# An adaLN block with a spectral network and a SwiGLU network: the gate modulation and the first gate weights are computed inside the first network, and its last shrunk rows and first output rows come in another order

## The chip, the cores and the metric

One core of a Trainium2 chip runs the whole program. The metric is the device time of one execution in microseconds (us). Three executions of the kernel before were timed, and its figure is their median, 1454.27 us. A profile comes from one further execution, recorded by the hardware profiler. The engines are named as in the profile: PE is the matrix engine and PEld its weight loads, DVE the vector engine, ACT the scalar (activation) engine, POOL the GpSimd engine and SP the engine that here only issues DMAs. SPq, ACTq and POOLq are the DMA queues of those engines.

## The reference

The input x has 4096 tokens (one row of a 1 x 4096 image) of 640 channels, all in float32. With silu(a) = a * sigmoid(a):

```
mod = (silu(c) @ w_mod).reshape(c.shape[0], 6, 1, -1)
sa, ca, ga, sb, cb, gb = mod[:, 0], mod[:, 1], mod[:, 2], mod[:, 3], mod[:, 4], mod[:, 5]
h = layernorm(x) * (1 + ca) + sa
x = x + ga * A(h)        # first network
h = layernorm(x) * (1 + cb) + sb
x = x + gb * B(h)        # second network
```

A is a spectral network: a real FFT over the 4096 tokens, a complex two-layer perceptron in four blocks of 160 channels on each frequency (ReLU between the layers), a soft shrinkage by 0.01 of the real and the imaginary parts, and the inverse FFT. B is SwiGLU: (silu(h @ w_gate) * (h @ w_up)) @ w_down, with 1728 hidden columns. c is one row of 640 values, so each of the six modulations is one row of 640 values. In this text they are numbered m = 0 to 5: sa, ca, ga, sb, cb, gb. The last, gb, is the gate modulation of the title.

## The kernel before

Matrix products whose float32 inputs have to be kept exact are split: an operand becomes a rounded high part, copied by ACT, and a low part, which is the operand minus the high part, formed by DVE. Three matmuls (high by high, low by high, high by low) then take the place of one.

**First network.** The FFT is done as matmuls with DFT tables. The middle of the network runs over 8 chunks of frequencies with 4 steps each, 32 steps p = 0 to 31 that are written out by hand in program order; each engine works through its own instructions in this order. `LAST` is 28, the first step of the last chunk. In one step, `stage_l1` and `tail_l1` do the first layer of a block, `stage_l2` the second layer of the block before, and a row of frequencies that is a few steps older is moved by DMA (`move_x`), shrunk (`shrink`, on DVE, two operations at L812 and L813 in the last chunks), split (`shrink_high` on ACT at L819, `shrink_low` on DVE at L824), multiplied by the first inverse table (`stage_i`, L835 to L837), copied by ACT (L838) and stored to a scratch array `s2` in DRAM by POOL's queue (L839). Rows are counted in the same numbers as steps; the last loop handles rows 24 to 26, and rows 25 to 27 are finished behind it. Rows 28 to 31, of the last chunk, go another way: `shrink_last` and `inverse_last`, whose copies `cz` are stored by ACT's queue for the first half of the channels (hf = 0) and by POOL's for the second (hf = 1).

**Modulations.** The rows of w_mod are loaded in 5 pieces of 128 x 640 for each m. DVE multiplies piece k by a column of silu(c) and adds it up in the tile `acc` (`mod_add`, L553 and L555); then `mod_sum` sums over the partitions by matmuls against ones. For m = 0, 2, 3, 4 this is put into the loop over p by the tables `mods` and `sums`, five pieces in every six steps. m = 1 is done ahead of the loop. m = 5 (gb) is not in the loop: `gate_load`, `gate_add`, `gate_sum` and `gate_out` (L1595 to L1619) do it at the start of the second network.

**First output rows.** Behind the loop, `first_y(i, hf)` forms the outputs of the first four rows i = 0 to 3 of tokens for the two halves hf of the channels: matmuls with the table `et` against the rows read back from `s2` (`cfrm`, `cfrr`; L1035 for hf = 0, L1040 for hf = 1) and against `tt` (L1038, hf = 1). DVE multiplies by ga, POOL or DVE adds x, and `first_stats` and `first_norm` give the normalised rows `xn`. The order of the eight is the list `order` at L1069. After them come `inverse_last` for hf = 1 (L885), the 20 transposes of `xn` (L1890), and `first_g`.

**Second network.** The 4096 tokens are 6 tiles; tile 0 has 512 token columns. For each tile the hidden columns are worked off in blocks of 256: a gate block, an up block, and so on, with the remainder of 64 columns of both as a third set. The sets of weights of tile 0 are numbered n in the order gate 0, up 0, remainder, gate 1, up 1, gate 2, ...; `load_w` loads set n into a raw tile r0_n (L1375, or L1378 and L1379 for the remainder) by SP, and `prep_w` makes its high (L1393) and low (L1396) parts in wb0_n, of which there are two buffers. `first_g` (L1884) evaluates set 0: it splits the transposed rows into ht (high, L1892, and low, L1895, by way of hx, L1894) and runs 30 matmuls of 512 columns. The following sets are run by `plain` (L1942 to L1944). A row of weights of w_down (`wdr`) is multiplied by gb on POOL (`fold`, L1559) and split. Beside this, tile 0 finishes the rest of the first network's output, row by row (r = 4, 5, ...: `row_load`, L1659 chh, L1662 chl, the matmuls py at L1672).

Here the order is not written by hand. A planner builds it while the program is generated: pieces of work are `Step`s with an engine, an estimated duration, the keys that they need and the buffers that they take; they stand in chains, and the planner puts the next step of a chain in place when its estimated time on its engine comes. `core("A", t)` and `core("V", t)` tell it how long ACT and DVE are taken by work outside the chains.

## Time and profile before

| | |
|---|---|
| three timed executions | 1447.88, 1454.27, 1458.53 us |
| median | 1454.27 us |
| profiled execution, its own time | 1457.64 us |
| its span, from the first to the last instruction | 1455.9 us |
| mean granted clock of PE | 0.995 |
| PE busy | 1410.7 us, 97% |
| DVE, ACT, POOL busy | 1089.2, 785.8, 543.6 us |
| DMA, mean | 260 GB/s |

Times in the views below are microseconds from the start of the span. A row of a timeline gives the start, the duration, the engine, the line, the operation and the tiles (out<-in); x7 at its end is the number of instructions put together in the row, and a bracket gives the idle time of the engine just before it and what ended it. The second network starts at about 312 us, where the transposes of `xn` begin, and the first down projection (`pd`) of tile 0 starts at 354.56 us.

### The profile page before, as it was taken

The numbers are of one execution on the slowest core, as the hardware profiler recorded it, in microseconds if no ns is written. First come the engines' busy times: TensorE is split into PE (matmuls) and PEld (weight loads), VectorE is DVE, ScalarE is ACT, GpSimd is POOL, SyncE is SP. The second block draws the span as 40 slices with busy tenths as digits, with TensorE's granted clock in tenths as the row PEclk, the third lists the DMA queues.
The fourth block names the chain that finished last, engine by engine and source line by source line (L and its number), as shares of the span: only waits on it lengthen the run. The fifth ranks groups of instructions, "written<-read, shape, count | busy, mean of one in ns | idle before, by whom it ended". The sixth has DMA issues, their size and how long they took to land.

```text
span 1455.9 us, 23927 instructions
## 1 busy us (share of the span) xinstructions
PE 1410.7 (97%) x8516; PEld 1331.4 (91%) x8516; DVE 1089.2 (75%) x1974; ACT 785.8 (54%) x1559; POOL 543.6 (37%) x640
## 2 busy tenths in 40 slices
PE   6899999988999999999999999999999999999998
PEld 2699999856888888899999999999999999999998
DVE  8868777768787788757878868778747767567775
ACT  7858888644544555544565456555435445244432
POOL 5300100145545344322544423444324545046532
PEclk9999999999999999999999999999999999999999
DMA  9978677557677988798987997877796666966652
GB/s 379 319 239 256 205 210 234 182 185 237 224 280 259 333 302 276 277 371 288 314 271 250 347 377 253 302 246 242 241 350 215 219 218 239 351 210 233 205 186 86
DMA packets 186136, 379.00 MB, mean 260 GB/s; under 512 B 22145, under 2 KB 104001, under 8 KB 184225
## 3 DMA queue, kind: packets, MB, share of 16 engines
q1 hardware_dynamic: 177824, 361.09, 72.4%
q0 software_dynamic: 6608, 13.77, 3.0%
q10 hardware_dynamic: 1584, 2.62, 0.5%
q8 instruction: 67, 1.10, 0.3%
q14 instruction: 53, 0.43, 0.1%
HBM read 263.39 MB, written 104.86 MB: 253 GB/s over the span
## 4 chain that ended last, share of the span: by engine, by line
PE 75%; DVE 10%; DMA 7%; ACT 3%; issue 2%; POOL 2%; SPq 1%; DVEq 0%; ACTq 0%; POOLq 0%
PE pd L2399 13%; PE pw L2078 8%; PE pw L2080 8%; PE pw L2079 7%; PE pc L777 4%; PE pd_X L2259 4%; PE pl L709 4%; PE pg L1942 2%; PE pg L1943 2%; PE pg L1944 2%; PE pd_Y L2259 2%; PE pw L2089 2%; PE pw L2091 2%; PE pw L2090 2%; DMA cr<-s 2%
## 5 line engine op out<-in xcount | busy, mean ns | idle before, releaser
L2399 PE MATMUL pd<-wdh,a 128*128 128x320 f32 x1040 | 239.2, 310 | 1.4 <-DVE x L2371 0.8
L2399 PEld LDWEIGHTS pd<-wdh,a 128*128 128x128 f32 x1040 | 176.2, 188 | 2.6 <-DVE x L2371 1.0
L1396 DVE TENSOR_TENSOR wb<-r,wb 128x512 fp32r<-128x512 f32 (+3 forms) x156 | 160.3, 1035 | 19.4 <-ACT wb L1393 17.3
L2399 PE MATMUL pd<-wdl,a 128*128 128x320 f32 x540 | 166.2, 309 | 0.0
L2078 PE MATMUL pw<-h,wt 128*128 128x384 f32 x416 | 141.0, 339 | 2.0 <-ACT s_y L2097 1.2
L2080 PE MATMUL pw<-h,wt 128*128 128x384 f32 x416 | 140.4, 337 | 0.0
L2079 PE MATMUL pw<-h,wt 128*128 128x384 f32 x416 | 139.9, 336 | 0.0
L2371 DVE TENSOR_TENSOR x<-x,pd 128x320 f32<-128x320 f32 x240 | 109.0, 478 | 37.8 <-PE pd L2399 33.9
L1393 ACT ACTIVATE wb<-r 128x512 fp32r<-128x512 f32 (+3 forms) x172 | 117.9, 703 | 34.4 <-PE pw L2091 24.9
L2080 PE MATMUL pw<-h,wb 128*128 128x384 f32 x312 | 105.1, 337 | 2.3 <-DVE wb L1396 2.3
L2078 PE MATMUL pw<-h,wb 128*128 128x384 f32 x312 | 105.3, 337 | 0.0
L2079 PE MATMUL pw<-h,wb 128*128 128x384 f32 x312 | 104.8, 336 | 0.0
L1942 PE MATMUL pg<-ht,wb 128*128 128x512 f32 x260 | 103.6, 398 | 1.3 <-ACT wb L1393 1.3
L1944 PE MATMUL pg<-ht,wb 128*128 128x512 f32 x260 | 102.2, 393 | 2.2 <-DVE wb L1396 2.2
L1943 PE MATMUL pg<-ht,wb 128*128 128x512 f32 x260 | 102.0, 392 | 0.0
L2399 PEld LDWEIGHTS pd<-wdl,a 128*128 128x128 f32 x540 | 101.4, 188 | 0.5
L2097 ACT ACTIVATE s_x<-pw 128x384 f32<-128x384 f32 x52 | 25.4, 489 | 114.0 <-PE pw L2080 113.3
L1655 POOL TENSOR_TENSOR cr<-cr,gab 128x640 f32<-128x640 f32 x28 | 48.0, 1715 | 98.6 <-DMA cr<-s 89.6
L839 POOL DMA_DIRECT2D s<-co x28 | 15.7, 562 | 181.8 <-ACT co L838 174.0
L2078 PEld LDWEIGHTS pw<-h,wt 128*128 128x128 f32 x416 | 78.4, 188 | 3.7 <-ACT s_y L2097 2.3
L2079 PEld LDWEIGHTS pw<-h,wt 128*128 128x128 f32 x416 | 78.5, 189 | 0.0
L2080 PEld LDWEIGHTS pw<-h,wt 128*128 128x128 f32 x416 | 78.3, 188 | 0.0
(346 smaller groups left out, 4057.6 us busy)
## 6 DMA issues: line engine op xcount, KB each, us to landing
wt<-td SPq DMA_DIRECT2D x104, 512.0 KB, 5.3
hs<-ho SPq DMA_DIRECT2D x52, 512.0 KB, 4.9
h<-hs SPq DMA_DIRECT2D x32, 768.0 KB, 9.3
r<-in_B_w_gate_dram SPq DMA_DIRECT2D x36, 640.0 KB, 5.2
r<-in_B_w_up_dram SPq DMA_DIRECT2D x36, 640.0 KB, 5.4
wdr<-wdd SPq DMA_DIRECT2D x21, 640.0 KB, 5.1
td<-wt SPq DMA_DIRECT2D x25, 512.0 KB, 5.8
g<-s SPq DMA_DIRECT2D x7, 1280.0 KB, 7.6
```

Source lines behind the costliest of these rows:

```text
L709: mm(pls[g][:, :NN], *seqs[g][i], start=(i == 0), stop=(i == n - 1))
L1393: act.activation(wbs[t, n][:, 0, ks, e], raw[t, n][:, ks, e], AF.Copy)
L1396: (pool if onp else dve).tensor_tensor(wbs[t, n][:, 1, ks, e], raw[t, n][:, ks, e], f32(wbs[t, n][:, 0, ks, e]), op=OP.subtract)
L1942: mm(b, wh, hh, start=(kk == 0), stop=False)
L1943: mm(b, wh, hl, start=False, stop=False)
L1944: mm(b, wl, hh, start=False, stop=(kk == 4))
L2078: mm(b, w(0, kp), a[:, kp, 0], start=start and kp == 0, stop=False, skip_group_check=not start)
L2079: mm(b, w(0, kp), a[:, kp, 1], start=False, stop=False, skip_group_check=not start)
L2080: mm(b, w(1, kp), a[:, kp, 0], start=False, stop=kp == 1, skip_group_check=not start)
L2259: mm(bk[b, i][:, :320], x, y, start=new and j == 0, stop=j == len(seq) - 1, skip_group_check=not new)
L2371: dve.tensor_tensor(x2[:, e], x2[:, e], x[0][:, :320], op=OP.add)
L2399: mm(pd[g, hf][0][:, :320], l, m, start=i == 0, stop=i == len(s) - 1 and not (last and len(gs) > 1))
```

## The change

It has four parts.

1. The modulation gb (m = 5) joins the other four in the loop of the first network. The pieces come one in each step from p = 2 on (loads) and p = 4 on (adds), where they came five in six steps; the sums stand at p = 9, 14, 19, 24 and 29, and the two halves of ga are now summed in the same step. The gate steps of the second network go.
2. The first gate weights (set 0) are loaded a second time, early: `first_gate` at p = 30 loads them by SP into two raw tiles (wr4, wr1) behind the load of x2_0. `first_gate_high` makes the high parts on ACT behind the loop, `first_gate_low` the low parts on DVE ahead of the first output rows. `first_g` uses these. wb0_0 is not made any more; its raw tile r0_0 is still loaded, since sums of weights for later tiles are formed from it, but behind r0_1 and r0_2. Two of the five hx tiles are made by DVE in place of ACT, and the planner is told 5.6 and 5.3 us in place of 7.7 and 7.4.
3. Row 27 is shrunk on POOL at p = 30 (`shrink_pool`) in place of DVE behind the loop, and at p = 31 the splits of row 26 and the high part of row 27 are moved forward, around `tail_l1`.
4. The list `order` has another order, and the statistics and norms of rows move with it.

The core of the diff:

```diff
+            gbb = []
...
-            for i, m in enumerate((0, 2, 3, 4)):
+            for i, m in enumerate((0, 2, 3, 4, 5)):
                 for k in range(5):
-                    mods.setdefault(3 + 6 * i + k, []).append((mod_load, m, k))
-                    mods.setdefault(5 + 6 * i + k, []).append((mod_add, m, k))
-                sums.setdefault(11 + 6 * i if m < 4 else LAST, []).append((mod_sum, m, 1))
-                if m == 2:
-                    sums.setdefault(10 + 6 * i, []).append((mod_sum, m, 0))
+                    mods.setdefault(2 + 5 * i + k, []).append((mod_load, m, k))
+                    mods.setdefault(4 + 5 * i + k, []).append((mod_add, m, k))
+                if m in (2, 5):
+                    sums.setdefault(9 + 5 * i, []).append((mod_sum, m, 0))
+                sums.setdefault(9 + 5 * i, []).append((mod_sum, m, 1))
...
+            def first_gate():
+                src = wg.rearrange("(k p) f -> p k f", p=P)
+                wraw.append(hp.tile([P, 4, 256], F32, tag="rz", bufs=2, name="wr4"))
+                wraw.append(p2.tile([P, 256], F32, tag="wm", bufs=1, name="wr1"))
+                nc.sync.dma_start(wraw[0], src[:, 0:4, 0:256])
+                nc.sync.dma_start(wraw[1], src[:, 4, 0:256])
+            def first_gate_high():
+                for k in range(5):
+                    act.activation(wh[k], wraw[0][:, k] if k < 4 else wraw[1], AF.Copy)
+            def first_gate_low():
+                for k in range(5):
+                    dve.tensor_tensor(wl[k], wraw[0][:, k] if k < 4 else wraw[1], f32(wh[k]), op=OP.subtract)
+            def shrink_pool(n):
+                xx = xxs[n // 4, n % 4]
+                pool.tensor_scalar(acc, xx, LAM, -LAM, op0=OP.min, op1=OP.max)
+                pool.tensor_tensor(xx, xx, acc, op=OP.subtract)
...
             for p in range(LAST + 1, NP):
+                last = p == NP - 1
...
+                if last:
+                    on(shrink_high, p - 5)
+                    on(shrink_low, p - 5)
                 on(tail_l1, p)
+                if last:
+                    on(shrink_high, LAST - 1)
...
                     load_first()
-                on(shrink_high, p - 5)
+                    first_gate()
+                    shrink_pool(LAST - 1)
...
-            on(shrink, LAST - 1)
-            on(shrink_high, LAST - 1)
+            first_gate_high()
             on(stage_i, LAST - 2)
...
-            order = [(0, 1), (1, 1), (0, 0), (1, 0), (2, 0), (3, 0), (2, 1), (3, 1)]
+            order = [(0, 1), (1, 1), (2, 1), (0, 0), (1, 0), (2, 0), (3, 0), (3, 1)]
...
-                    act.activation(x, pts[k], AF.Identity, bias=sb1[:, k:k + 1], scale=cb1[:, k:k + 1])
+                    if k < 3:
+                        act.activation(x, pts[k], AF.Identity, bias=sb1[:, k:k + 1], scale=cb1[:, k:k + 1])
+                    else:
+                        dve.tensor_scalar(x, pts[k], cb1[:, k:k + 1], sb1[:, k:k + 1], op0=OP.mult, op1=OP.add)
...
-                core("A", 7.7)
-                core("V", 7.4)
+                core("A", 5.6)
+                core("V", 5.3)
```

What it does to the order of the instructions is shown at three places. The first is PE among the first output rows, before; py0_i_hf is the output of row i and half hf.

```order
L1040 MATMUL py0_1_1_3837<-cfrm_3085,et_3284 128x320
L1035 MATMUL py0_0_0_3846<-cfrm_3085,et_3284 128x320
L1035 MATMUL py0_1_0_3851<-cfrm_3085,et_3284 128x320
L1035 MATMUL py0_2_0_3863<-cfrr_3086,et_3284 128x320
L1035 MATMUL py0_3_0_3875<-cfrr_3086,et_3284 128x320
L1038 MATMUL py0_2_1_3880<-tt7_0_3547,et_3284 128x320 x2
L1038 MATMUL py0_2_1_3880<-tt7_1_3558,et_3284 128x320 x2
L1040 MATMUL py0_2_1_3880<-cfrr_3086,et_3284 128x320
```

And the same place of the changed program:

```order
L1082 MATMUL py0_1_1_3879<-cfrm_3104,et_3303 128x320
L1080 MATMUL py0_2_1_3888<-tt7_0_3575,et_3303 128x320 x2
L1080 MATMUL py0_2_1_3888<-tt7_1_3586,et_3303 128x320 x2
L1082 MATMUL py0_2_1_3888<-cfrr_3105,et_3303 128x320
L1077 MATMUL py0_0_0_3897<-cfrm_3104,et_3303 128x320
L1077 MATMUL py0_1_0_3902<-cfrm_3104,et_3303 128x320
L1077 MATMUL py0_2_0_3912<-cfrr_3105,et_3303 128x320
L1077 MATMUL py0_3_0_3924<-cfrr_3105,et_3303 128x320
```

The five matmuls of row 2's second half moved ahead of the four outputs that read the first half of `cfrm` and `cfrr`.

The second place is SP's queue between the two networks, before; r0_n are the raw weight tiles, gwm the pieces of w_mod for gb, wdr the first rows of w_down, cr4 and x4 the inputs of row 4.

```order
L1375 DMA r0_0_3944<-in_B_w_gate_dram 128x5x256
L1375 DMA r0_1_3965<-in_B_w_up_dram 128x5x256
L1378 DMA r0_2_3967<-in_B_w_gate_dram 128x5x64
L1379 DMA r0_2_3967<-in_B_w_up_dram 128x5x64
L1597 DMA gwm0_3952<-in_w_mod_dram 128x640
L1597 DMA gwm1_3971<-in_w_mod_dram 128x640
L1597 DMA gwm2_3973<-in_w_mod_dram 128x640
L1597 DMA gwm3_3975<-in_w_mod_dram 128x640
L1597 DMA gwm4_3953<-in_w_mod_dram 128x640
L1552 DMA wdr0_0_3959<-in_B_w_down_dram 128x2x640
L1375 DMA r0_3_4065<-in_B_w_gate_dram 128x5x256
L1375 DMA r0_4_4085<-in_B_w_up_dram 128x5x256
```

After the change the same queue reads (the tiles named cr0_0 and x0_0 hold row 4's inputs):

```order
L1417 DMA r0_1_3994<-in_B_w_up_dram 128x5x256
L1420 DMA r0_2_3987<-in_B_w_gate_dram 128x5x64
L1421 DMA r0_2_3987<-in_B_w_up_dram 128x5x64
L1417 DMA r0_0_4009<-in_B_w_gate_dram 128x5x256
L1594 DMA wdr0_0_4002<-in_B_w_down_dram 128x2x640
L1650 DMA cr0_0_3995<-s2 128x640
L1646 DMA x0_0_3996<-in_A_x_dram 128x640
L1417 DMA r0_3_4116<-in_B_w_gate_dram 128x5x256
L1417 DMA r0_4_4118<-in_B_w_up_dram 128x5x256
L1613 DMA wdd<-wdr0_0_4002 128x1280
L1650 DMA cr5_4161<-s2 128x640
L1646 DMA x5_4170<-in_A_x_dram 128x640
```

The five gwm loads are gone, r0_0 stands behind r0_1 and r0_2, and row 4's inputs moved ahead of r0_3. Of the two buffers of its tag, r0_3 takes the one that r0_0 had in the program before, and so waits for the low part of wb0_0; now it takes that of r0_2, and waits for the low part of wb0_2.

The third place is ACT behind `first_g`, before; sg are the silus of the first gate block, wb0_n the high parts, a0 the high part of silu times up, wt the summed weights for later tiles, chh4 the high part of row 4.

```order
L1964 ACTIVATE sg0_0_0_3962<-pg0_0_3984 128x512
L1964 ACTIVATE sg0_0_1_4070<-pg0_1_3985 128x512
L1393 ACTIVATE wb0_1_4072<-r0_1_3965 128x512
L1393 ACTIVATE wb0_1_4072<-r0_1_3965 128x768
L1393 ACTIVATE wb0_2_4083<-r0_2_3967 128x2x128
L1450 ACTIVATE wt0_0a_3951<-ts0_3950 128x2x256
L1393 ACTIVATE wb0_2_4083<-r0_2_3967 128x3x128
L1619 ACTIVATE gbb_3960<-gpm0_4116 128x320
L1619 ACTIVATE gbb_3960<-gpm1_4118 128x320
L1978 ACTIVATE a0_0_0_0_3954<-sg0_0_0_3962 128x512
```

And after the change:

```order
L1435 ACTIVATE wb0_1_3982<-r0_1_3994 128x512
L1435 ACTIVATE wb0_1_3982<-r0_1_3994 128x768
L1973 ACTIVATE sg0_0_0_4004<-pg0_0_4013 128x512
L1973 ACTIVATE sg0_0_1_4095<-pg0_1_4014 128x512
L1435 ACTIVATE wb0_2_4102<-r0_2_3987 128x2x128
L1435 ACTIVATE wb0_2_4102<-r0_2_3987 128x3x128
L1606 ACTIVATE wdh0_0_4003<-wdr0_0_4002 128x640 x2
L1987 ACTIVATE a0_0_0_0_3997<-sg0_0_0_4004 128x512
L1666 ACTIVATE chh4_4153<-cr0_0_3995 128x640
L1435 ACTIVATE wb0_3_4168<-r0_3_4116 128x512
L1435 ACTIVATE wb0_3_4168<-r0_3_4116 128x768
```

The high parts of the second set moved ahead of the two silus, the copies of gb are gone from here, and row 4's high part stands ahead of the fourth set instead of behind it. On PE the six matmuls py of row 4 moved with it: before they stood between the two halves of the fourth set (pg0_3_0 and pg0_3_1), now they stand inside the remainder set, pg0_2_0.

96 lines of the change are left out of this document (38 added, 58 removed).

## The prediction

> **What bounds the kernel now.** I read the span on the page, then the windows by stage, then the waits of PE where the change works, then the timelines at those places.
>
> ```profile
> span 1455.9 us, 23927 instructions
> 72.00:258.00 186.00, 183.53 (x1415) 181.54 (x1415) 144.76 (x275) 148.08 (x304) 14.92 (x38) 0.99 0.75 230
> 258.00:312.00 54.00, 50.35 (x297) 42.21 (x298) 38.45 (x80) 24.91 (x55) 12.70 (x23) 1.00 0.43 139
> 312.00:355.00 43.00, 34.62 (x143) 25.94 (x140) 32.27 (x36) 22.81 (x40) 21.16 (x22) 0.92 0.78 255
> 355.00:450.00 95.00, 93.48 (x506) 82.69 (x504) 77.70 (x118) 47.93 (x82) 52.36 (x50) 1.00 0.74 253
> ```
>
> Behind the span, the four rows are stretches: the loop of the first network, its end, the start of the second network up to the first down projection, and the rest of tile 0. After each length come the busy times of PE, PEld, DVE, ACT and POOL, PE's granted clock, the DMA share and GB/s. PE is idle 2.5 us of 186 in the loop, 3.65 of 54 at the end, 8.4 of 43 at the start of the second network and 1.5 of the next 95. So PE bounds the whole, and a change that does not cut matmuls has about 12 us to win in the two middle stretches, plus what the clock of 0.92 costs there. PE's waits of these stretches:
>
> ```profile
> PE pg L1944 <- DVE wb L1396: 2.2, 2, 1.4
> PE py L1672 <- DVE chl L1662: 2.2, 1, 2.2
> PE pg L1904 <- DVE ht L1895: 1.5, 1, 1.5
> PE pg L1942 <- ACT wb L1393: 1.3, 1, 1.3
> PE pi L836 <- DVE xl L824: 1.1, 1, 1.1
> PE py L1035 <- DMA cfrm<-s: 1.1, 1, 1.1
> PE gpm L1616 <- DVE gacc L1604: 0.7, 1, 0.7
> PE pi L835 <- ACT xh L819: 0.7, 1, 0.7
> ```
>
> Each row gives what PE waited for, the total, the times and the longest. The change touches every one of them.
>
> **The order of the first output rows: -1.1.** The 1.1 us on `cfrm` falls on the first hf = 0 output, behind (1,1). Now (2,1) stands there: five matmuls, half of this row of eight and half of the next of two, or 1.5 us.
>
> ```profile
> 303.57 2.32 PE L1038 MATMUL py<-tt,et 128*128 128x320 f32 x8
> 305.72 0.70 PE L1040 MATMUL py<-cfrr,et 112*128 112x320 f32 x2
> ```
>
> They need nothing that lands later, so 1.5 covers 1.1 and the wait goes. The row statistics that end last stay those of row 3, at the same place.
>
> **The end of the first network: 0.** The waits on `xh` and `xl`, 1.8 us together, are what a faster shrink of row 27 could win. But DVE is the bound there, in an unbroken run from the landing of the moved rows up to the `xl` that PE waits for:
>
> ```profile
> 269.12 5.82 DMA xx<-tt
> 285.23 0.82 DVE L824 TENSOR_TENSOR xl<-xx,xh 128x640 fp32r<-128x640 f32 x1
> 285.96 0.49 DVE L812 TENSOR_SCALAR cl<-xx 128x640 f32<-128x640 f32 x1
> 286.10 0.41 PE L836 MATMUL pi<-xl,bm 128*128 128x320 f32 x1 [1.07 <-DVE xl L824]
> ```
>
> Row 27's shrink (0.49 for its first half, shown last but one) stood behind that `xl`, so taking it off DVE shortens nothing ahead of it. Row 26's split is earlier in the code, but its `stage_i` needs a bank that ACT's copy of row 25 frees, and that copy now queues behind row 27's high part, which itself waits until row 25's inverse is done. I count 0, between -1.8 (both waits go) and +2.0. The upper end is the work that enters DVE's run: POOL now shrinks beside it. What that costs has a near row:
>
> ```profile
> 313.98 2.58 DVE L1396 TENSOR_TENSOR wb<-r,wb 128x512 fp32r<-128x512 f32 x2 [0.73 <-ACT wb L1393]
> 327.22 1.69 DVE L1396 TENSOR_TENSOR wb<-r,wb 128x512 fp32r<-128x512 f32 x2 [4.55 <-ACT wb L1393]
> 316.48 3.49 DVE L1895 TENSOR_TENSOR ht<-hx,ht 128x512 fp32r<-128x512 f32 x3
> 321.51 0.69 DVE L1895 TENSOR_TENSOR ht<-hx,ht 128x512 fp32r<-128x512 f32 x1 [0.65 <-ACT hx L1894]
> 314.99 0.74 POOL L1440 TENSOR_TENSOR ts<-r 128x256 f32<-128x256 f32 x1
> 318.24 1.18 POOL L1440 TENSOR_TENSOR ts<-r,ts 128x256 f32<-128x256 f32 x1
> L1559 POOL TENSOR_TENSOR wdr<-wdr,gbb 128x640 f32<-128x640 f32 x14 | 24.7, 1787 | 31.8 <-ACT gbb L1619 14.6 <-DMA wdr<-in_B_w_down_dram 14.0 <-DVE mv_b L1684 3.2
> ```
>
> The same pair of DVE subtractions took 2.58 beside POOL and 1.69 without it; three others took 3.49 where 3 x 0.69 is 2.1. So DVE lost 2.3 us beside POOL's four operations (the first and the last are shown), 4.4 us from the first start to the last end: half. POOL's shrink is two operations on 128x640; the last row has 1.79 for one, so 3.6 us, half of which is 1.8, in a run of DVE with little room to hide it. That 1.8 stands against the gains of the reordering, which is why I put them at 0 together. The Trainium skill, "SBUF — State Buffer", section "SBUF: two separate sides", says the port pair that VectorE and GpSimd share is an exclusive lock, and that the loser blocks fully for the whole instruction. By it the price would be up to 3.6 and this part +1.8. The rows above, at a half, lie between that and no contention at all.
>
> **The first gate product: -2.1, of which the clock 1.4.** PE's rows here:
>
> ```profile
> 312.52 2.56 PE L1890 MATMUL pt<-idn,xn 128*128 128x128 f32 x20
> 319.78 0.63 PE L1904 MATMUL pg<-ht,wb 128*128 128x512 f32 x1
> 320.21 0.63 PE L1902 MATMUL pg<-ht,wb 128*128 128x512 f32 x1
> 325.38 0.39 PE L1903 MATMUL pg<-ht,wb 128*128 128x512 f32 x1
> 325.60 0.39 PE L1904 MATMUL pg<-ht,wb 128*128 128x512 f32 x1
> ```
>
> In the 10.9 us from the end of the transposes (315.1, first row) to the end of the product (326.0, last row), PE runs 30 matmuls that at full pace start 0.23 apart: 6.9. The rest is the waits of 0.4 on ht's high and 1.5 on its low part, and seven matmuls in a slow stretch, of which the second and third rows are two. Starts 0.43 apart against 0.23: seven times 0.2 is 1.4. wb0_0's split (on DVE the 2.58 above) goes from ahead of ht, so ACT starts on ht as soon as the transposes are there. But the first low part still needs two ACT copies (1.34 for two, since DVE waited 0.65 for them behind its own 0.69 above) and a subtraction of 0.69, so 2.0 in all, against which PE has a start after the first copy, at 0.7, and two matmuls: 0.8 to 1.1 of the wait remains. I count 0.7 of the 1.9 of waits as gone, and 1.4 for the clock, if the slow stretch goes with them. The early splits have these gaps:
>
> ```profile
> 287.39 0.74 ACT L819 ACTIVATE xh<-xx 128x640 fp32r<-128x640 f32 x1 [2.03 <-issue]
> 289.96 0.83 ACT L838 ACTIVATE co<-pi 128x320 f32<-128x320 f32 x2 [1.18 <-PE pi L837]
> 297.60 0.49 DVE L1044 TENSOR_TENSOR acc<-py,gab 128x320 f32<-128x320 f32 x1 [2.38 <-PE py L1040]
> ```
>
> ACT is idle for 2.0 + 1.2 us, DVE for 2.4. Five copies of 256 columns are 1.5 us by ACT's 0.74 for 640 in proportion, 3.7 at the most; five subtractions 1.7 by DVE's 0.69 for 512, 3.5 at the most. By the middle of each they fit and cost nothing; at the upper ends 0.5 to 1.1 shows, which is in the bounds of the last part.
>
> **The second set: -0.8.** PE waited 1.3 for wb0_1's high part, since ACT did two silus first, and those need the end of the product. Now the high parts come first; the raw tile is loaded earlier. What I leave, 0.5, is DVE's low part behind it.
>
> **The gate sum: -2.0.** Its wait of 0.7 and this row's 1.3 go from tile 0:
>
> ```profile
> 332.62 1.31 PE L1616 MATMUL gpm<-gacc,ones 128*128 128x320 f32 x4 [0.73 <-DVE gacc L1604]
> L555 DVE SCALAR_TENSOR_TENSOR acc<-wm,sc,acc 128x640 f32<-128x640 f32 x16 | 14.0, 876 | 0.0
> ```
>
> The matmuls return at p = 29, around 270 us, where PE runs ahead of DVE: DVE's run begins at the landing of the moved rows, and PE waits 1.8 for it later, so 1.3 fits. The five adds of 0.88 return in the loop: 4.4 us on DVE, which is busy 145 of 186 there, while PE hardly waits. I count +0.5, between 0 and 4.4.
>
> **The fourth set, row 4 and the second slow stretch: -2.2, -2.2, -1.4.** PE's waits of 2.2 on wb0_3's low part and 2.2 on chl had one cause: DVE did the gacc adds first, and the later splits followed late. With the adds gone, and row 4's loads and high part ahead, both should be there in time. Behind those two waits come the matmuls of another slow stretch:
>
> ```profile
> 349.73 0.63 PE L1942 MATMUL pg<-ht,wb 128*128 128x512 f32 x1
> 352.29 0.58 PE L1942 MATMUL pg<-ht,wb 128*128 128x512 f32 x1
> ```
>
> The first and the last of seven, 0.43 apart: again 1.4. That both slow stretches go rests on the assumption that they follow from the waits ahead of them. The Trainium skill, "TensorE: Matmul & The Clock Gate", Part 1, says the clock halves after an idle window of about 3.4 us. No single wait here is longer than 2.2, so by that rule the stretches are not owed to these waits and would stay. This is a rival below.
>
> **What is given back: +2.8.** POOL's first fold waited 14.6 us for gbb (the idle time in its row above); it will now run right behind the load of wdr, beside DVE's low parts of sets 1 and 2. Two operations are 3.6 us, half is 1.8, less some idle time of DVE: +1.3, between 0 and 3.6. And a PE that is earlier meets loads that are not: I take +1.5 for new waits in tile 0, between 0 and 6 (what is won in 312 to 355 without the clock).
>
> **Sum.** -1.1 - 2.1 - 0.8 - 2.0 - 2.2 - 2.2 - 1.4 = -11.8; +0.5 + 1.3 + 1.5 = +3.3; **-8.5**. The profiled execution took 1457.64, so 1449.1; the median of the runs, 1454.27, is 3.4 below it, so **1445.8**. Within 1%, about what a measurement of this kernel can tell from no change, is 1439.7 to 1468.8.
>
> **The rivals.**
>
> *The cover only moves.* DVE is busy 32 of 43 us at the start of the second network and 38 of 54 before; PE's waits there are nearly all for DVE. If DVE and POOL's lock take back what the adds leave (the lock 3.6 in place of 1.3, new waits 4.0 in place of 1.5, and 1.0 at the end of the first network), 5.8 goes: -2.7, **1451.6**. For it speaks the half pace beside POOL; against it, that 4.4 us of adds leave.
>
> *The clock stretches stay.* Without 2 x 1.4: -5.7, **1448.6**. For it: the stretches follow waits of 0.4 and 1.5 and of 1.4, 0.9 and 2.2, all short.
>
> *All waits go and nothing comes back.* -11.8, and the end of the first network wins its 1.8: -13.6, **1440.7**. Against it stands DVE's unbroken run.
>
> *Slower: SP's queue.* The load of r0_3 now waits for DVE's low part of wb0_2, which waits for ACT's high part behind both silus, so it is issued about 3 us after the first gate product. Behind it on SP stand r0_4, the store wdd, row 5's inputs and all later sets. PE needs wb0_3 after 30 matmuls of set 1 (6.9), 15 of the remainder (3.4) and the six py (1.5), 11.8 behind the product; less 3.0 and a split of 1.3, the load may take 7.5. These are its landings:
>
> ```profile
> r<-in_B_w_gate_dram SPq DMA_DIRECT2D x4, 640.0 KB, 7.3
> r<-in_B_w_gate_dram SPq DMA_DIRECT2D x36, 640.0 KB, 5.2
> ```
>
> 7.3 is the median of the four of this place, 5.2 that of the whole program. It decides from 7.5 on. If each of the 11 sets from n = 3 on came late by the difference, 2.1, it would be +23.1 - 8.5 = +14.6, **1468.9**. Against it: the five gwm loads of 320 KB, which stood in the queue where 7.3 was measured, are gone.
>
> *It does not do what it says.* r0_0 is still loaded, so set 0 is not saved but read twice, 640 KB more; the early copy goes at about 276 us, where the stretch's DMA share is 0.43. Its price is nothing unless it delays the moved rows behind it.
>
> **How the numbers follow.** The forecast has 0.48, the cover that moves 0.20, the clock that stays 0.14, all waits gone 0.10, the queue 0.08. The range holds the first four with the open bounds: 1438, which is all waits gone less half of its distance from the forecast (2.6), to 1460, the forecast with the adds (3.9 more), the lock (2.3 more) and new waits (4.5 more) at their upper bounds, 1456.5, and the profiled execution's excess of 3.4. Faster by over 1% needs -14.6, only the far side of "all gone": 0.09. Slower by over 1%: 0.08. Within: 0.83.
>
> **What would show it.** The wait on `cfrm` gone; L1035's successor starting without idle time; between 312 and 355 PE idle under 4 us in place of 8.4, and the clock above 0.97; no gpm; wb0_3 and chl without a wait. Wrong if DVE's low parts of sets 1 to 3 take over 1.0 each beside the fold, if PE waits at `xl` for over 3 us, or if r0_3 lands over 7.5 us after its issue.

## The result and the profile after

The changed kernel takes 1461.06 us (median of 15 runs, 1454.68 to 1465.93), the kernel before 1454.27 (15 runs). The ratio is 1.0048, with a 95% interval of 1.0036 to 1.0061: 6.8 us slower. Forecast were 1445.8 us and a range of 1438 to 1460. So the sign was wrong, and the time lies just outside the range.

A single profile hides this. The profiled execution of the change spans 1455.5 us, 0.4 less than that of before, because the first is a quick execution of its kernel and the other a long one. Each kernel was therefore profiled once more. The windows of the second profile of before, and then those of the change's first profile, for the stretches of the prediction and a later one (after the length: busy time of PE, PEld, DVE, ACT, POOL, then PE's clock, DMA share, GB/s):

```profile
258.00:312.00 54.00, 51.08 (x299) 42.45 (x300) 38.73 (x81) 25.85 (x58) 13.63 (x25) 1.00 0.47 153
312.00:355.00 43.00, 34.64 (x165) 27.30 (x165) 35.78 (x42) 24.44 (x42) 23.12 (x22) 1.00 0.80 264
355.00:450.00 95.00, 93.70 (x504) 82.86 (x503) 77.95 (x125) 47.12 (x80) 52.47 (x50) 1.00 0.74 254
700.00:1030.00 330.00, 326.70 (x2023) 323.26 (x2022) 257.83 (x472) 181.76 (x371) 138.28 (x163) 1.00 0.81 280
```

```profile
258.00:312.00 54.00, 50.05 (x291) 41.63 (x289) 41.68 (x82) 26.99 (x63) 15.07 (x25) 1.00 0.47 149
312.00:355.00 43.00, 40.01 (x196) 33.18 (x197) 36.00 (x49) 24.67 (x41) 24.29 (x26) 0.96 0.67 230
355.00:450.00 95.00, 90.19 (x473) 79.11 (x472) 72.06 (x116) 44.46 (x77) 46.39 (x48) 0.98 0.75 253
700.00:1030.00 330.00, 323.32 (x2002) 319.87 (x2001) 261.64 (x473) 182.57 (x373) 135.72 (x164) 1.00 0.83 286
```

Three things are to be seen. From 312 to 355 PE is busy 40.0 us in place of 34.6, as forecast. From 355 to 450 it is idle 4.8 us in place of 1.3, and from 700 to 1030 6.7 in place of 3.3. And the second profile of before has a clock of 1.00 from 312 to 355, where the first had 0.92: the two slow stretches there are in one execution and not in the next, so they can't be counted in full as something that an edit wins.

The waits of PE in the change from 258 to 450 us (what waited, for what, total, times, longest):

```profile
PE pt L1743 <- ACT xn L1710: 3.6, 1, 3.6
PE py L1679 <- DVE chl L1669: 2.5, 2, 1.6
PE pi L888 <- ACT cz L889: 1.8, 1, 1.8
PE pi L839 <- DVE xl L827: 1.0, 2, 0.5
PE py L1082 <- DMA cfrm<-s: 0.7, 1, 0.7
PE pg L1913 <- DVE ht L1905: 0.7, 1, 0.7
```

Of the old waits those for the second set, the fourth set and gb's sum are gone, and so is the 1.1 on `cfrm` at the first output with hf = 0. The 0.7 on `cfrm` here is another wait: it stands at the very first output, (0,1), where the profile of before had none. Of the 2.5 on chl, 1.6 fall on row 4, in place of 2.2; in the second profile of the change row 4 does not wait for chl. Two waits have come: 1.8 on `cz` (0.5 before) and 3.6 on a row's xn.

I cut the program at two points that every profile shows: the first transpose `pt` and the first down projection `pd`. In the kernels whose parts around a point are the same, the profiles agree within a few us, so several can be put together (mean, and lowest to highest; "old" in the first row are before, twice, and three experiments with the same first network; "new" are the change, twice, and five experiments that share its first network).

| stretch | old | new | difference | forecast |
|---|---|---|---|---|
| start to the first transpose | 310.9 (308.7 to 312.5; 5 profiles) | 315.8 (313.9 to 317.6; 7 profiles) | +4.9 | -0.6 |
| first transpose to first `pd` | 39.9 (38.8 to 42.0; 3 profiles) | 31.7 (31.2 to 32.7; 3 profiles) | -8.2 | -9.4 |
| first `pd` to the end | by difference | by difference | +10.1 | +1.5 |
| all, from the timed runs | | | +6.8 | -8.5 |

The last stretch is what is left of 6.8. Single profiles point the same way, with a wide spread: 1101.1 and 1101.3 from `pd` to the end of the span for before, 1108.9 and 1117.7 for the change. The old 39.9 contains the 42.0 of the profile with the two slow stretches; against the other two old profiles (38.8 and 38.9) the middle is -7.1, where the forecast without its clock terms was -6.6, and the last stretch is +9.0. So the middle came out as forecast. The first network lost what was forecast as neutral, the lead at `pd` was worth nothing at the end of the program, and more was lost besides.

### The profile page after: what moved, and what is told of

It reads as the page before. It is cut to its first block, busy times and chain, and to the rows that moved or that the text cites. A ratio compares the mean times of both kernels' runs of the same rounds, so it can differ in the third digit from the quotient of the medians.

```text
span 1455.5 us, 23934 instructions
## 1 busy us (share of the span) xinstructions
PE 1408.3 (97%) x8516; PEld 1329.5 (91%) x8516; DVE 1093.4 (75%) x1977; ACT 785.0 (54%) x1560; POOL 538.6 (37%) x642
## 4 chain that ended last, share of the span: by engine, by line
PE 70%; DVE 12%; DMA 9%; ACT 3%; issue 3%; POOL 2%; SPq 1%; DVEq 0%; POOLq 0%; ACTq 0%
PE pd L2408 12%; PE pw L2087 8%; PE pw L2089 8%; PE pw L2088 8%; PE pd_X L2268 4%; PE pl L712 4%; PE pc L780 4%; PE pd_Y L2268 2%; PE pw L2098 2%; PE pw L2100 2%; PE pw L2099 2%; PE pb L616 2%; DMA cr<-s 2%; DVE wb L1438 2%; DVE st_a L192 2%
```

## The experiments

In the table, "ratio" is that of the timed runs to runs of before on the same chip, with its interval, and "us" is the ratio put into us of 1454.5. "first pt" and "first pd" are from one profile each.

| kernel | ratio | us | first pt | first pd |
|---|---|---|---|---|
| change | 1.0048 (1.0036 to 1.0061) | +7.0 | 313.9, 315.7 | 346.6, 346.9 |
| part 4 alone | 1.0015 (1.0002 to 1.0029) | +2.2 | 311.1 | 352.1 |
| part 1 alone | 1.0019 (1.0001 to 1.0036) | +2.8 | 311.6 | 350.5 |
| part 2 alone | 1.0038 (1.0026 to 1.0050) | +5.5 | 310.5 | 349.8 |
| change, planner's old numbers | 1.0060 (1.0041 to 1.0080) | +8.7 | 315.3 | 350.8 |
| change, old order of the second network | 1.0026 (1.0012 to 1.0039) | +3.8 | 316.5 | 352.4 |
| before, planner's new numbers | 0.9982 (0.9965 to 0.9999) | -2.6 | 310.9 | 349.5 |
| change without part 4 | 1.0022 (1.0006 to 1.0037) | +3.2 | 314.6 | 345.9 |
| change without part 3 | 1.0037 (1.0017 to 1.0058) | +5.4 | 315.2 | 346.3 |
| parts 1 and 2, old order | 1.0002 (0.9988 to 1.0016) | +0.3 | 314.8 | 350.1 |
| parts 1 and 2, order of the new numbers | 0.9999 (0.9983 to 1.0015) | -0.1 | 312.7 | 344.2 |

### The parts one by one

Part 4 alone is the three edits to `order`, `first_stats` and `first_norm` of the diff, put on the kernel before.

> The kernel before with the fourth part alone: the new order of the first output rows, with the statistics and norms that go with it. The second network's order is untouched. Theory A (the change's own places gain what was forecast, and the loss comes from the second network's new order): the wait on cfrm goes, 1454.3 - 1.1 = 1453.2. Theory B (the loss comes from the end of the first network): this part alone is slower, 1456 or more.

Measured 1.0015. Theory A's gain of 1.1 did not come, and theory B was right in sign. The waits of PE in this kernel, 258 to 316 us:

```profile
PE pi L885 <- ACT cz L886: 1.8, 1, 1.8
PE pi L836 <- DVE xl L824: 1.1, 1, 1.1
PE pg L1902 <- ACT ht L1892: 0.4, 1, 0.4
```

The `cfrm` wait is gone here (as it is, without part 4, in the second profile of before), and `cz` has gone from 0.5 to 1.8. That 1.8 is in every profile of a kernel with part 4, and 0.5 in those without. ACT's and PE's rows in the change show how it arises:

```profile
308.88 0.92 ACT L1106 ACTIVATE xn<-x,sa,ca 128x640 f32<-128x640 f32 x1 [13.18 <-POOL sa L1100]
311.00 0.92 ACT L1106 ACTIVATE xn<-x,sa,ca 128x640 f32<-128x640 f32 x1 [1.20 <-POOL sa L1100]
311.82 0.74 ACT L889 ACTIVATE cz<-pi 128x320 f32<-128x320 f32 x2
...
309.18 1.35 PE L888 MATMUL pi<-tt,bx 64*128 64x320 f32 x8
312.29 1.67 PE L888 MATMUL pi<-tt,bx 64*128 64x320 f32 x8 [1.76 <-ACT cz L889]
```

The second norm stands ahead of the `cz` copies on ACT and starts at 311.0, since row 1's statistics now end two outputs later; in the second profile of before, the two norms were over by 307.9, ahead of `pi` at 308.4. The copies were ready to start when PE had its first `pi` results, at about 310, and PE needs the banks that they free.

> The changed kernel without its fourth part (old order of the first output rows). The second network's order is that of the change. Theory C (part four costs: its norms stand ahead of the cz copies on ACT, a wait of 1.8 in place of 0.5, which also leaves the clock low at the transposes): from the first output row to the transposes 17 to 18 us in place of 18.8 to 19.6, total 1458 to 1459.5. Theory D (part four is neutral and the second network alone loses): 1461 within 1.

Measured 1.0022 against 1.0048: taking part 4 out of the change gives back 0.0026, or 3.8 us with an uncertainty of about 2.9 (from the two intervals). Theory C holds. From the first `py` to the first transpose this profile has 17.7 us; the seven profiles with all of the new first network have 18.8 to 20.4, the five old ones 17.3 to 18.4.

Part 1 alone: the new tables `mods` and `sums` with m = 5, and the gate steps removed.

> The kernel before with the first part alone: gb's sum inside the first network, its steps gone from the second. This changes what the planner sees, so the second network's order changes too. Theory A: the stretch from 312 to the first down projection gets shorter by 3 to 5 us, and tile 0 gives it back later at waits for the row's xn or for the w_down pieces; total 1452 to 1460 by where the planner's order falls. Theory B (five more adds on DVE in the loop): the loop ends 2 to 4 us later, and the total is 1456 to 1459.

Measured 1.0019, inside the ranges of both theories. The first output row starts at 294.9, against 291.3 to 294.6 in the old profiles, so one profile shows little of theory B's 2 to 4 us in the loop. All profiles together show them, at the last `pl` (a first-layer matmul of the loop's last step): it starts at 277.9 to 280.8 us in the seven profiles of kernels without part 1, and at 281.3 to 284.5 in the thirteen with it, 2.8 later on the mean. The four matmuls of gb's sum, 1.3 us, are in this. Of theory A's 3 to 5 us nothing came: from the first transpose to `pd` it is 38.8, as in the second profile of before.

Part 2 alone: `first_gate` and its splits, `first_g` with them, the planner's two numbers; gb is summed in the second network as before.

> The kernel before with the second part alone: first gate weights loaded and split early, gb still summed in the second network. Theory A: the first gate product ends 2 to 3 us earlier, and what follows depends on the planner's new order: 1450 to 1460. Theory B: the end of the first network pays for the early splits on ACT and DVE and for 640 KB more, and this part alone is slower, 1457 or more, with the loss ahead of 312 us.

Measured 1.0038, but not where theory B put it: the first transpose is at 310.5, as in before. The first `pd`, at 349.8, is no real lead either: row 4's six matmuls py, which stand ahead of it in the other kernels, come behind it here. The loss is all behind.

Part 3 out of the change:

> The changed kernel without its third part (row 27 shrunk on DVE, the old last step). Theory C (POOL's shrink beside DVE's unbroken run delays the first output rows): first output row at 294 in place of 295.1 and 296.1, total 1459.5 to 1460.5. Theory D: 1461 within 1.

Measured 1.0037 against 1.0048, a difference of 0.0011 with an uncertainty of 0.0024. What POOL's shrink costs is not told apart from nothing by the times, and the first output row came at 295.4, not at theory C's 294. The profiles show some 0.7 us: from the last `pl` to the first output row it is 13.6 to 13.7 us in the eight profiles with part 3, and 12.7 to 13.3 in the five with part 1 but without part 3.

### Is it the planner's order?

Parts 1 and 2 change the order of the second network far beyond their own place, so the first suspicion fell on the planner.

```diff
-                core("A", 5.6)
-                core("V", 5.3)
+                core("A", 7.7)
+                core("V", 7.4)
```

> The changed kernel with the two numbers told to the planner for ACT and DVE beside the first gate product back at 7.7 and 7.4. All work is the same, only the planner's order in the second network moves. Theory A: the time moves by more than 3 us from 1461 (to 1450 to 1458 if the new numbers put steps into a bad order), with the first network unchanged. Theory B: 1461 within 2 us, since the loss is elsewhere.

Measured 1.0060, a median of 1462.76, which is theory B's figure; it is slower by 0.0012 than the change, with an uncertainty of 0.0023. Another order of the same work, and not a better one. That the loss is elsewhere does not follow, since this order is not that of before either.

The same two numbers the other way round, in the kernel before, and nothing else:

> The kernel before with the planner's two numbers beside the first gate product at 5.6 and 5.3 in place of 7.7 and 7.4, nothing else: same work, but another order of the second network at some 240 places of DVE's rows. Theory A: 5 to 9 us slower than before (1459 to 1464), with the same first 312 us. Theory B: 1454.5 within 2 us.

Measured 0.9982 (0.9965 to 0.9999). Theory A falls here: the new numbers do not make a bad order, in the kernel before they make a slightly better one. It is the only kernel of this study that is ahead of before, by 2.6 us, at the edge of what the runs can tell.

Then the change with an order like that of before. The planner still goes through the gate steps and the first split in its books, without an instruction:

```diff
+            def ghost(steps):
+                for st in steps:
+                    st.f = lambda: None
+                return steps
...
-            for _ in prep_w(0, 0):
+            for _ in ghost(prep_w(0, 0)):
```

> The changed kernel, all four parts as they are, but the planner is told of the steps of the kernel before (the gate steps and the first split are gone through in its books without any instruction, with the numbers 7.7 and 7.4), so that the second network's order is that of before apart from the removed instructions. Theory A (the changed order of the second network costs what the first network and the start of the second gain): first down projection near 348, and the time from there to the end as before, 1098 us in the profile: in all 1446 to 1450. Theory B (the gain is given back whatever the order, because row chain and w_down supply do not come earlier): 1453 to 1458, with new waits in 355 to 450.

Measured 1.0026, 3.2 us less than the change, with an uncertainty of 2.7. So the order costs something, but its return does not bring the forecast: the time is at the upper end of theory B's. The first transpose is at 316.5 and the first `pd` at 352.4: this kernel pays for the first network and has little of the early start, because the old order holds the second set's splits behind the silus.

Without parts 3 and 4, with the old order and with that of the kernel at 0.9982:

> Parts one and two alone, and the planner told of the steps of before, so that the second network keeps the order of before. Theory E (parts one and two gain at the start of the second network as forecast, parts three and four lose at the end of the first, and the new order of the second network loses the rest): transposes at 312, first down projection at 346 to 349, from there 1101 to 1104 as in the two profiles of before, total 1448 to 1452. Theory F (whatever is gained early is given back because later work is paced by loads): 1454 to 1458.

> As the run before, but with the planner's numbers 5.6 and 5.3 in the books, so that the second network has the order that the kernel before took with these numbers (1451.9 measured). Theory E: 1446 to 1450, faster than before by 0.3% to 0.5%. Theory F: 1452 to 1456.

Measured 1.0002 and 0.9999. Theory E's forecasts (1448 to 1452 and 1446 to 1450) did not come, theory F's did. The ledger then reads, from the ratios: parts 1 and 2 with the old order +0.3 us, parts 3 and 4 on top +3.5 (1.0026 against 1.0002), the new order on top +3.2 (1.0048 against 1.0026), each with 2 to 3 us of uncertainty. Alone, each with the order that the planner makes for it, parts 1 and 2 cost 2.8 and 5.5; together, in two other orders, nothing. So most of what each costs alone seems to go with its order, but both parts in the planner's own order for them were not run.

PE's idle time in the profiles goes with the order too. From 355 to 450 us it is 3.8 to 7.2 in the seven profiles with the order of the change (mean 5.4), and 0.5 to 2.9 in the seven with that of before (mean 1.6), whatever the first network is. From 700 to 1030 the means are 7.6 and 5.7, and 1.9 in the three profiles with the order of the kernel at 0.9982.

### Where the early start goes

The last kernel has the same order of the second network as the one at 0.9982, so their rows can be laid beside each other. PE and DVE of that kernel (planner's new numbers, nothing else), then of the one with parts 1 and 2:

```profile
334.19 1.36 DVE L1568 TENSOR_TENSOR wdl<-wdr,wdh 128x640 fp32r<-128x640 f32 x1
335.47 0.68 DVE L1974 TENSOR_TENSOR sg<-pg,sg 128x512 f32<-128x512 f32 x1
...
349.47 0.30 PE L2399 MATMUL pd<-wdh,a 128*128 128x320 f32 x1
397.42 0.87 DVE L1683 BATCH_NORM_STATS2 st_b<-x 128x6 f32<-128x320 f32 x2
412.73 0.27 PE L1736 MATMUL pt<-idn,xn 128*128 128x128 f32 x1
```

```profile
334.22 1.36 DVE L1598 TENSOR_TENSOR wdl<-wdr,wdh 128x640 fp32r<-128x640 f32 x1
335.50 0.68 DVE L1990 TENSOR_TENSOR sg<-pg,sg 128x512 f32<-128x512 f32 x1
...
344.24 0.30 PE L2415 MATMUL pd<-wdh,a 128*128 128x320 f32 x1
396.02 0.87 DVE L1697 BATCH_NORM_STATS2 st_b<-x 128x6 f32<-128x320 f32 x2
411.12 0.27 PE L1750 MATMUL pt<-idn,xn 128*128 128x128 f32 x1
```

PE is 5.2 us ahead at `pd` and 1.6 at a transpose of tile 0's second half. DVE is not ahead at all at 335, and 1.4 at 396, though five adds and a split had been taken from it. A part of that is that this kernel's first transpose comes 1.8 later, and that DVE makes two hx tiles here, 0.8 each. What else keeps it is seen in the rows before, first of the kernel at 0.9982, then with parts 1 and 2:

```profile
324.02 0.96 DVE L1396 TENSOR_TENSOR wb<-r,wb 128x768 fp32r<-128x768 f32 x1 [0.37 <-ACT wb L1393]
324.89 1.80 DVE L1604 SCALAR_TENSOR_TENSOR gacc<-gwm,sc,gacc 128x640 f32<-128x640 f32 x2
326.61 0.89 DVE L1396 TENSOR_TENSOR wb<-r,wb 128x256 fp32r<-128x256 f32 x2
```

```profile
325.47 5.14 DVE L1426 TENSOR_TENSOR wb<-r,wb 128x768 fp32r<-128x768 f32 x3 [2.22 <-ACT wb L1423]
326.21 3.98 POOL L1589 TENSOR_TENSOR wdr<-wdr,gbb 128x640 f32<-128x640 f32 x2
```

The three subtractions (one of 768 columns, two of 256) take 0.96 + 0.89 = 1.85 in the first and 5.14 in the second, where POOL's fold of 3.98 runs beside them: 3.3 us lost. The fold used to wait for gb; with gb early it starts with its data and falls on DVE's splits. In the other kernel it falls on later operations (chl at 1.86 and `a` at 2.06, where this kernel has 0.81 and 1.22), so its earlier place costs 1.4 net. DVE was also idle for 2.2 us ahead of the splits. In the change the fold (3.40 from 325.1 on) falls on two splits of 256 columns, 2.81 in place of 0.89, and row 4's multiplication and a weight sum on POOL fall on one subtraction, 3.17 beside 0.81 for its pair:

```profile
328.81 3.17 DVE L1610 TENSOR_TENSOR wdl<-wdr,wdh 128x640 fp32r<-128x640 f32 x1
332.51 0.81 DVE L1610 TENSOR_TENSOR wdl<-wdr,wdh 128x640 fp32r<-128x640 f32 x1
```

Laid over the other kernel instruction by instruction, DVE is 1.1 to 2.7 us ahead from 341 to 403 us and 0.8 from 409 on, and PE's lead of 5.2 goes down to that: 2.7 at 366, 2.1 at 387, 0.8 at 413. Its waits show that DVE's results hold it: in the kernel with parts 1 and 2, PE waits from 344 to 414 us for

```profile
PE pd L2415 <- DVE x L2387: 2.7, 1, 2.7
PE pt L1750 <- ACT xn L1717: 2.4, 2, 1.2
PE py L1686 <- DVE x L2387: 0.8, 1, 0.8
```

and its windows 326 to 336 and 336 to 406 show DVE at 10.0 of 10 us and 61 of 70 (columns as above), so it is full in the first and not in all of the second:

```profile
326.00:336.00 10.00, 9.11 (x41) 7.27 (x41) 10.00 (x10) 3.71 (x7) 7.60 (x7) 1.00 0.72 205
336.00:406.00 70.00, 64.80 (x335) 55.95 (x334) 61.14 (x92) 32.63 (x55) 35.59 (x37) 0.98 0.77 266
```

If PE's lead at `pd` is worth nothing, then taking it away must cost nothing. First I delayed the whole start of tile 0, by doing the transposes four times:

```diff
                     for k in range(5):
-                        pe.transpose(pts[k][:, 128 * i:128 * i + 128], xns[0][i][:, 128 * k:128 * k + 128], idn)
+                        for _ in range(4):
+                            pe.transpose(pts[k][:, 128 * i:128 * i + 128], xns[0][i][:, 128 * k:128 * k + 128], idn)
```

> The changed kernel with each of the 20 transposes ahead of the first gate product done four times (the same values), which is 60 x 0.128 = 7.7 us more of PE at that place and nothing else: the order of everything stays. Theory F (what is gained at the start of the second network is given back, because later work is paced by supply): the first down projection comes at about 353, but from there to the end 1104 to 1107 in place of 1109 to 1118; total 1461 to 1464. Theory G (the rest is slower for its order alone): the whole 7.7 shows, 1467 to 1470.

> The kernel before with the same delay. Theory F: it has little to give back in tile 0 (PE waited 1.5 us from 355 to 450), so 5 to 8 us of the 7.7 show, 1459.5 to 1462. Theory G: all 7.7, 1462.

Measured 1.0074 and 1.0053. In before all of it shows (0.0053 is 7.7 us), in the change 0.0026, 3.8 us with an uncertainty of 3.4. The change, at 1464.3, lies just above theory F's range; before, at 1462.9, is no nearer to one theory than to the other. But a delay there holds back ACT, DVE and the load of w_down's rows too, which all start from the transposes.

So the second delay adds work to PE alone, at a later place: the 30 matmuls of the fourth set are done a second time, right ahead of `pd`.

```diff
+                    if (t, n) == (0, 3):
+                        for kk in range(5):
+                            hh, hl = (ht[t, kk][:, i] for i in range(2))
+                            wh, wl = (wb[:, i, kk, 128 * f:128 * f + 128] for i in range(2))
+                            mm(b, wh, hh, start=(kk == 0), stop=False)
+                            mm(b, wh, hl, start=False, stop=False)
+                            mm(b, wl, hh, start=False, stop=(kk == 4))
                     if k == "s":
```

> The changed kernel with the 30 matmuls of the fourth set done twice (the same values), 6.8 us more of PE just ahead of the first down projection; all else and the order as in the change. Unlike the delay at the transposes it holds back nothing but PE: the splits, folds and loads of the other engines can run on. Theory F (PE's lead there is worth nothing, since DVE and the row chain do not come earlier): 0 to 3.5 us of the 6.8 show, 1461 to 1464.5. Theory G (the lead is kept, and the order loses): 5 to 7 show, 1466 to 1468.

> The same 6.8 us in the kernel with parts one and two alone and the order of the second network that the kernel before takes with the planner's numbers 5.6 and 5.3. In the profiles its lead over that kernel, 5.2 us at the first down projection, was down to 0.8 at 413 us. Theory F: 0 to 3 us show, 1455.5 to 1458.5. Theory G: 5 to 7, 1460.5 to 1462.5.

Measured 1.0043 against 1.0048 without the delay, and 1.0003 against 0.9999: -0.7 us with an uncertainty of 2.8, and +0.6 with 3.5, of 6.8 us of added work. The first `pd` moved by 7.4 us, as the rows of the change and of the delayed kernel show (1.8 of it was there at the first transpose):

```profile
346.58 0.30 PE L2408 MATMUL pd<-wdh,a 128*128 128x320 f32 x1
```

```profile
353.95 0.30 PE L2415 MATMUL pd<-wdh,a 128*128 128x320 f32 x1
```

That is theory F: by the timed runs, 6.8 us of PE at this place are worth nothing at the end, to within some 3 us, in two kernels. The profiles show this for one of them: in the kernel with parts 1 and 2 the delay is 7.8 at `pd`, 2.1 at 409 us, 5 again from 420 to 558, 1.0 at 606 and 2.4 at the end of the span. For the change they do not: the delayed kernel's DVE too is 5 to 8 us later than in the change's first profile from 348 us on, and the end of the span is 7.2 behind it; against the second profile, it is 1.9 ahead. Single executions differ by as much, which is why the timed runs decide here. The kernel before was not delayed in this way, so it is not shown that there such a lead would have lasted.

### Is it w_down's rows?

The wait of 3.6 on xn at 415 us follows a chain in the change: DVE's split of a w_down row stands ahead of a row's statistics and waits for ACT, which waits for POOL's fold and the load of the row.

```profile
409.74 1.42 DVE L1610 TENSOR_TENSOR wdl<-wdr,wdh 128x640 fp32r<-128x640 f32 x1 [2.53 <-ACT wdh L1606]
411.08 0.87 DVE L1690 BATCH_NORM_STATS2 st_b<-x 128x6 f32<-128x320 f32 x2
```

There is one raw tile for these rows, and each load waits for the store of the fold before. To cut this, the store was taken from the split's high part:

```diff
-                    nc.sync.dma_start(wdd[p], wdraw[t, p].rearrange("p a b -> p (a b)"))
+                    nc.sync.dma_start(wdd[p], f32(wds[t, p][0].rearrange("p a b -> p (a b)")))
```

> The changed kernel with the store of the folded w_down rows taken from their high part in place of the raw tile, so that the next load of w_down rows does not wait for the store to land (later tiles read the high part only; the low part of the folded rows is left out there). Same order, same amount of DMA. Theory F with w_down as the supply: the loads of tile 0 come 3 to 6 us earlier each, the wait of the transposes on xn (2.9 to 3.6) and the slow clock behind it go, total 1452 to 1457. Theory G: 1461 within 1.5.

> The kernel before with the same store from the high part. Theory F with w_down as the supply: it gains less than the changed kernel does, 0 to 2 us (1452.5 to 1454.5), since PE is later there and hardly waits from 355 to 450. Theory G: 1454.5 within 1.5.

Measured 1.0033 and 1.0009. (The low part of the folded rows, which later tiles would read, is left out by these kernels.) The third load of tile 0 is issued 3.8 us behind the store in place of 8.0 in both profiles of the change, so there the store's landing had held it; the fourth 5.4 behind it in place of 5.9 and 6.4. Counted from the first transpose the third comes 2 to 4 us earlier and the fourth not. The wait on xn is still 3.0. So the landing of the store is not what paces tile 0. The kernel is perhaps 2 us faster than the change (0.0015, uncertainty 0.0021), which is not told apart from nothing. The 3 us wait on xn itself belongs to the order: it is 2.9 to 3.7 in seven profiles with the order of the change, with and without parts 3 and 4, with the delay at the transposes or without.

### The second profiles

> The kernel before once more, for a second profile: the profiled one was 3.4 us over the median. Both theories: 1450 to 1459, and fewer slow stretches of the clock if the time is near the median.

> The changed kernel once more, for a second profile: the profiled one was 3.8 us under the median. Both theories: 1457 to 1466; theory A puts its losses at the same waits of the second network as in the first profile.

Measured 1453.51 and 1466.41. The first has a clock of 1.00 in the stretch from 312 to 355. The second loses at the same waits as the first (3.4 on xn, 1.8 on `cz`), and more in the middle of the program.

## Why the prediction was wrong, point by point

**What bounds the kernel.** "PE bounds the whole" is right as a mean and was the root of the error. DVE was 78 of 95 us busy from 355 to 450, and I read the 17 us left as room. In some stretches of 10 us it has none (10.0 from 396 to 406 in the same profile), and much of what PE waits for comes from it. The mean share itself does not tell: in the change DVE is busy less from 355 to 450, 72 and 74 us, and PE waits more.

**The order of the first output rows, -1.1.** Wrong in sign. "They need nothing that lands later" was right of PE's matmuls, but the step did not follow what else moved: the norms went from the 4th and 5th output to the 6th and 7th, in front of ACT's `cz` copies. Measured +2.2 alone and +3.8 as part of the change. From the first output row to the first transpose the new profiles have 2.0 us more on the mean (19.7 against 17.7), 1.3 of it as the wait on `cz`. The `cfrm` wait that was to go went, but it is not a fixed 1.1: it is 0 in the second profile of before.

**The end of the first network, 0 between -1.8 and +2: right; the adds beside it, +0.5: too small.** The first output row starts at 296.1 on the mean of the seven new profiles and at 293.2 on that of the five old ones, +2.9. From the last `pl` of the loop to that row it is 13.6 us in both, so the end itself is neutral. The loss is ahead of it, in the loop: 2.8 us with part 1 (thirteen profiles against seven), inside the bounds of 0 to 4.4 but not the 0.5 that went into the sum. 1.3 of it are the four matmuls of gb's sum, which the prediction put at nothing because they would fit where PE runs ahead of DVE.

**The first product, the second set, the gate sum, the fourth set: right.** -8.2 us from transposes to `pd` (-7.1 without the slow stretches, for a forecast of -6.6), with the waits gone that were to go, except chl's in one of the two profiles. DVE's two hx tiles, 1.6 us, had no term. The rival of SP's queue did not come: r0_3's split is done without PE waiting for it.

**The clock, -2.8: wrong.** The two slow stretches were in one execution and not in the next of the same kernel. The Trainium skill, "TensorE: Matmul & The Clock Gate", Part 1, adds that the window in which activity is counted runs freely. The traces agree in this: the same waits came with a slow stretch in one profile and without in the next, and the windows of 312 to 355 give 0.92 and 1.00. Neither assumption held as it stood. Slow stretches do follow from waits, as the sum took it, and not from long idle windows alone; but a short wait brings one in some executions only. The 2.2 on chl has one behind it in four of the seven profiles with that wait. And the change brings waits of its own: a slow stretch begins behind the 1.8 on `cz` in eight of the nine profiles with part 4, and in or behind the 2.9 to 3.7 on xn in five of seven. In the timed runs the mean clock is 0.9965 for the change and 0.9978 for before (131 runs of the experiments). At 1.5 us for each 0.001, the trend of the 15 runs of the change, that is an estimate of 2 us of the 6.8.

**DVE beside POOL, +1.3 between 0 and 3.6.** The cause was named, and sized at a half. In the kernel with parts 1 and 2 DVE loses 3.3 us beside 4.7 us of POOL's work (the fold, and the end of row 4's multiplication ahead of it), seven tenths; less what the fold cost at its old place, it is 1.4. The rule of the Trainium skill, "SBUF — State Buffer", section "SBUF: two separate sides" (the loser of the shared port pair blocks fully), comes closer than the half that I took.

**Given back later, +1.5 between 0 and 6: the term that failed.** It measured +10.1 (+9.0 without the slow stretches of one old profile). Up to 7 of it is the lead that PE had at `pd`: that such a lead is worth nothing, to within some 3 us, is shown by the timed runs of the two kernels with more work on PE there. The cause that I give for it, that PE falls back to DVE's pace in tile 0, is read from the rows of two kernels in one order. It isn't tested by taking DVE's work away, and in the change itself the 3.6 on xn has DVE idle, for a split whose w_down row is late. About 3 is the new order of the second network, with its wait on xn (1.0048 against 1.0026 with the old one). I had bounded the term by what is won between 312 and 355; the order, which moved rows in all later tiles, had no term at all. The rival "the cover only moves" came nearest to the mechanism, and was given less than half of the forecast's chance and a price of 5.8 where it needed some 15.

## What to carry to other kernels

An engine that is busy four fifths of a stretch can still be full for the 10 us that matter. Before a saving on the bounding engine is counted to the end of the program, look at the second engine in windows as short as the saving: where it is full, the saving ends at its next result. More work put on one engine alone, at the place of the expected lead, prices such a lead, and the kernel before should get the same.

When an edit moves work past a planner or a queue, follow every engine's instructions that move, also those that "only come later" (here two norms of 0.9 us). And sum against the median, not against one profile: what a second execution doesn't show can't be counted in full.

## What the runs showed of the hardware

A DVE subtraction of 128x640 took 3.17 us beside POOL's work. Its pair took 0.81: it started 0.04 us ahead of a POOL operation of 128x256, and that one took 1.37 where another of its form took 0.74. Three DVE subtractions took 5.14 in place of 1.85 beside 4.7 us of POOL's. So here the one that starts second loses most of the other's time, more than the half that the profile of before suggested.

The slow stretches of PE's clock are 3.4 us long each, or twice that, at half the clock, and their number and place differ between executions of one program. In the 20 profiles there are 51 of them, those at the very end left out, and each begins during a PE wait of at least 1.0 us or within 2.3 us of its end. Of the PE waits from 75 us on, 11 of 13 of 2.6 us or more had one, 19 of 28 of 2.0 to 2.6, 12 of 46 of 1.5 to 2.0, and 5 of 119 of 1.0 to 1.5. In the 15 timed runs of the change the mean clock goes from 0.994 to 0.999, and the two ends of that took 1464.79 and 1454.68 us; so a part of the spread of some 11 us between runs goes with the clock.
